# Two-block decode attention on one core: V loads three units behind K loads, the last four V in pieces, the final transpose and scaling split by batch

## The chip, the cores and the metric

The kernel runs on one core of one Trainium2 chip. The metric is the device time of the slowest core in microseconds (us); with one core that is this core's time. Every run quoted here is fast (the runs of each kernel lie within 1.5% of its fastest), and every kernel gave the reference's result. "Span" is the length of the one profiled execution; it is 1.75 to 3.25 us shorter than the time taken of that same execution.

## The reference, cut to what matters

```python
# block A; block B is the same with its own inputs.  B=2 batches, 32 heads, Sk=8192, Dh=192, D=640, bf16
q = (x @ wq).reshape(B, 1, 32, 192).transpose(0, 2, 1, 3)
scores = einsum("bhqd,bhkd->bhqk", q, k_cache) * 192 ** -0.5
o = einsum("bhqk,bhkd->bhqd", softmax(scores), v_cache)
return o.transpose(0, 2, 1, 3).reshape(B, 1, 32 * 192) @ wo
# ... output: the two blocks' results side by side
```

One query per batch and head meets 8192 keys and values: 837 MB have to be read and hardly anything is reused, so this is a streaming problem.

## The kernel before: what the change and the argument touch

The work is cut in 128 units (2 blocks x 32 heads x 2 batches). A unit loads one K and one V tile, each 128 partitions x 24,576 bytes (3 MB), into two buffers each. VectorE multiplies K with the query and sums 48 of the 64 columns; ScalarE sums the other 16 with its accumulator; GpSimd finds the maximum over the partitions; ScalarE takes the exponential into `pb`; TensorE multiplies it with V in 32 matmuls ("PV"). Each pair of heads is then transposed by TensorE (f3), scaled by ScalarE (f4) and projected by TensorE (f5). Weights come in 16 groups, each a `wq` and a `wo` load of 960 KB.

All loads go through one queue, in this order; a K load waits until its buffer's product is done, a V load until its buffer's PV is done:

```python
for u in range(NU):
    korder.append(("k", u))
    if u >= 1:
        korder.append(("v", u - 1))
korder.append(("v", NU - 1))
# ... weights of the next group go in between, at u % 8 == 2 (wo) and 3 (wq)
```

The steady part of three engines is a loop; ahead of it and behind it the code is straight:

```python
LOOPS = dict(dve=[(6, 8, 15)], act=[(4, 8, 15)], pe=[(7, 4, 13), (71, 4, 13)])   # first slot, slots a turn, turns
```

At the end the last K comes in two parts, the last V in four pieces, ScalarE takes 26 columns instead of 16 in the last unit, and ten idle matmuls are there, meant to keep TensorE's clock up (in the trace of this kernel they run from 1940.8 to 1942.9 us; the granted clock is at half from 1941.88 and again from 1952.12, for 3.41 us each; what they do isn't shown).

## Time and profile before

| | before |
|---|---|
| time, median of 3 runs | 1969.08 us (1968.56 to 1969.44) |
| span of the profiled run | 1967.1 us |
| VectorE busy | 84% |
| DMA rate in the steady part | 430 to 431 GB/s |
| last part of the last V lands | 1953.76 us |
| last landing to the end of the span | 13.34 us |

The landing times are from the trace's records of the load semaphores: the trace has 16 updates for each load, and the profile counts 16 DMA engines. This document reads each update as one engine's part of the load; the trace doesn't name the engine. The kernel waits for all 16.

The first view is the profile page of the kernel before: busy time by engine, the data rate in 40 equal slices of the span, and the queues (packets, MB, share of the 16 engines' time).

```profile
PE 1120.1 (57%) x5014; PEld 593.3 (30%) x5014; DVE 1655.3 (84%) x962; ACT 905.0 (46%) x4763; POOL 133.2 (7%) x269
...
GB/s 384 429 429 430 431 430 431 429 431 431 427 433 431 430 431 429 433 430 431 429 429 431 429 430 431 430 432 427 433 430 430 432 429 431 431 429 431 431 430 286
...
q8 instruction: 11, 0.18, 0.0%
q14 instruction: 13, 0.11, 0.0%
```

The rate stands at 430 from the second slice to the last but one. No engine is busy all the time; the transfer is the limit. Note the last two lines, which look like nothing: 24 packets with which engines fetched their own instructions.

The table by stretch of the kernel before, one stretch of it: busy time of each engine with its count of instructions, granted clock, DMA share, GB/s.

```profile
core 0: us, PE busy (x) PEld busy (x) DVE busy (x) ACT busy (x) POOL busy (x), PEclk, DMA share, GB/s
...
1700.00:1900.00 200.00, 116.69 (x523) 61.66 (x522) 171.20 (x100) 95.72 (x504) 9.59 (x26) 0.74 1.01 431
```

The end of the chain of waits of the kernel before: start, duration, what, each step released by the one above it.

```profile
1901.70 22.52 DMA kb<-in_B_k_cache_dram
...
1940.93 8.98 ACT prodA L301 x52
...
1951.51 0.45 ACT pb L308 x2
...
1952.01 7.05 PE ops L382 x32
1959.06 1.15 PE oTps L401 x12
...
1961.53 0.92 PE outps L417 x6
...
1962.48 0.43 ACT oTz L337 x2
...
1962.95 1.77 PE outps L417 x6
...
1964.75 0.43 ACT out_sb L347
```

The last K is followed by its scores, by ScalarE's 26 accumulations (52 instructions, 8.98 us) and by the exponential at 1951.51. Only then can the 32 PV matmuls start, at 1952.01; the last part of V lands at 1953.76, while they run. So 13.34 us of this kernel lie behind the last byte. That is what the change goes for.

### The profile page before, as it was taken

What the parts mean: (1) busy time and instruction counts of PE and PEld (TensorE: products, weight loads), DVE (VectorE), ACT (ScalarE), POOL (GpSimd) and SP (SyncE); (2) the same over time, 40 slices, a digit from 0 to 9 for tenths busy, and PEclk for the clock granted to TensorE, in tenths of its full rate; (3) what the DMA queues carried; (4) which work ended last, traced back from release to release, by engine and by line L of the source; (5) the groups of instructions that cost most, each with busy time, mean ns of one, the idle gap of its engine ahead of it and who ended that gap; (6) DMA issues with size and microseconds to landing.
All of it is one profiled execution on the core that took longest, in us unless ns stands there. A gap on an engine that the chain in (4) does not pass through costs nothing.

```text
span 1967.1 us, 18620 instructions
## 1 busy us (share of the span) xinstructions
PE 1120.1 (57%) x5014; PEld 593.3 (30%) x5014; DVE 1655.3 (84%) x962; ACT 905.0 (46%) x4763; POOL 133.2 (7%) x269
## 2 busy tenths in 40 slices
PE   2565555655555565555654666556554565556557
PEld 1232223333232232332332333223332232323234
DVE  7787888888888888888888888888788888888886
ACT  4444544445445444454445444444444444544544
POOL 4020000000000000000000000000000000000001
PEclk7776777777777777777777777777777777777777
DMA  9999999999999999999999999999999999999996
GB/s 384 429 429 430 431 430 431 429 431 431 427 433 431 430 431 429 433 430 431 429 429 431 429 430 431 430 432 427 433 430 430 432 429 431 431 429 431 431 430 286
DMA packets 55896, 837.08 MB, mean 426 GB/s; under 512 B 7352, under 2 KB 18240, under 8 KB 22976
## 3 DMA queue, kind: packets, MB, share of 16 engines
q1 hardware_dynamic: 55856, 836.79, 99.6%
q8 instruction: 11, 0.18, 0.0%
q14 instruction: 13, 0.11, 0.0%
q10 hardware_dynamic: 16, 0.01, 0.0%
HBM read 836.77 MB, written 0.01 MB: 425 GB/s over the span
## 4 chain that ended last, share of the span: by engine, by line
DMA 75%; DVE 18%; issue 5%; PE 1%; ACT 1%; POOL 0%; SPq 0%; ACTq 0%; DVEq 0%
DMA kb<-in_B_k_cache_dram 38%; DMA kb<-in_A_k_cache_dram 37%; DVE prodD L283 16%; DVE prodD L290 1%; DVE prodA L279 1%; ACT prodA L301 0%; PE ops L382 0%; POOL mg L266 0%; DVE sc L294 0%; PE outps L417 0%; PE oTps L401 0%; SPq L219 0%; SPq L226 0%; ACT pb L308 0%; ACT out_sb L347 0%
## 5 line engine op out<-in xcount | busy, mean ns | idle before, releaser
L382 PE MATMUL ops<-vb,pb 128*33 128x384 bf16 x4096 | 957.9, 409 | 837.1 <-DMA vb<-in_A_v_cache_dram 421.5
L382 PEld LDWEIGHTS ops<-vb,pb 128*33 128x33 bf16 x4096 | 482.8, 120 | 1312.5 <-issue 674.4
L301 ACT ACTIVATE prodA<-prodA 128x192 bf16<-128x192 bf16 x2058 | 712.4, 350 | 76.1 <-DVE prodA L279 75.6
L283 DVE TENSOR_TENSOR prodD<-kb,qbc 128x9216 bf16<-128x9216 bf16 x128 | 632.7, 4943 | 3.5 <-DMA kb<-in_A_k_cache_dram 3.5
L290 DVE TENSOR_TENSOR prodD<-prodD 128x4608 bf16<-128x4608 bf16 (+2 forms) x384 | 598.1, 1558 | 13.3
L279 DVE TENSOR_TENSOR prodA<-kb,qbc 128x3072 bf16<-128x3072 bf16 x128 | 226.3, 1768 | 254.6 <-DMA kb<-in_B_k_cache_dram 127.8
L301 ACT ACTIVATION_READ_ACCUMULATOR prodA<-prodA 128x1 f32 x2058 | 390.4, 190 | 0.0
L305 ACT ACTIVATE nb<-mg 128x1 f32<-128x1 f32 x128 | 25.9, 203 | 704.8 <-POOL mg L266 704.8
L294 DVE TENSOR_REDUCE sc<-prodD 128x48 f32<-128x1152 bf16 x128 | 172.9, 1351 | 4.4
L266 POOL PARTITION_ALL_REDUCE mg<-mp x128 | 53.2, 416 | 1690.9 <-DVE mp L286 1690.9
L315 ACT ACTIVATE o_sb<-ops 1x384 f32<-1x384 f32 x63 | 30.2, 479 | 131.2 <-PE oTps L390 112.0
L343 ACT ACTIVATE qbc<-qps 128x384 bf16<-128x384 f32 x64 | 31.4, 491 | 119.5 <-PE qps L365 119.4
L270 POOL PARTITION_ALL_REDUCE lall<-rs x128 | 70.5, 551 | 115.3 <-ACT pb L308 115.3
L390 PEld LDWEIGHTS oTps<-ones,o_sb 33*128 33x128 f32 x372 | 67.1, 257 | 9.8 <-issue 9.8
L390 PE MATMUL oTps<-ones,o_sb 33*128 33x1 f32 x372 | 69.7, 311 | 0.0
L308 ACT ACTIVATE pb<-sc,nb 128x64 bf16<-128x64 f32 x128 | 52.2, 408 | 16.6 <-ACT nb L305 6.3
L286 DVE TENSOR_REDUCE mp<-sc 128x1 f32<-128x64 f32 x128 | 28.2, 220 | 14.2 <-issue 4.3
L365 PE MATMUL qps<-wqs,xbc_0 128*128 (+1 forms) x160 | 32.4, 334 | 6.2 <-DMA wqs<-in_A_wq_dram 6.2
L365 PE MATMUL qps<-wqs,xbc_1 128*128 (+1 forms) x160 | 32.2, 333 | 0.6 <-ACT qbc L343 0.6
L417 PE MATMUL outps<-wos,oTz 128*4 (+1 forms) x192 | 32.0, 304 | 0.5 <-ACT oTz L337 0.5
L316 ACT ACTIVATE o_sb<-ops 1x384 f32<-1x384 f32 x63 | 30.4, 482 | 0.7
L308 ACT ACTIVATION_READ_ACCUMULATOR pb<-sc,nb 128x1 f32 x128 | 23.9, 186 | 0.0
(29 smaller groups left out, 87.1 us busy)
## 6 DMA issues: line engine op xcount, KB each, us to landing
vb<-in_A_v_cache_dram SPq DMA_DIRECT2D x64, 3072.0 KB, 22.2
kb<-in_A_k_cache_dram SPq DMA_DIRECT2D x63, 3072.0 KB, 22.5
kb<-in_B_k_cache_dram SPq DMA_DIRECT2D x63, 3072.0 KB, 22.5
vb<-in_B_v_cache_dram SPq DMA_DIRECT2D x62, 3072.0 KB, 22.1
wos<-in_A_wo_dram SPq DMA_DIRECT2D x8, 960.0 KB, 24.5
wqs<-in_B_wq_dram SPq DMA_DIRECT2D x8, 960.0 KB, 26.8
wos<-in_B_wo_dram SPq DMA_DIRECT2D x8, 960.0 KB, 24.4
wqs<-in_A_wq_dram SPq DMA_DIRECT2D x7, 960.0 KB, 26.8
```

Source lines behind the costliest of these rows:

```text
L266: return lambda eng: eng.partition_all_reduce(mg[u % 2][:], mp[u % 2][:], 128, bass.bass_isa.ReduceOp.max)
L270: return lambda eng: eng.partition_all_reduce(lall[g % 2][:, b:b + 1], rs[u % 2][:], 128, bass.bass_isa.ReduceOp.add)
L279: return lambda eng: eng.tensor_tensor(prodA[u % 2][:, 0:na, :], kb[u % NK][:, 0:na, :], qb_bc(u, na), ALU.mult)
L283: return lambda eng: eng.tensor_tensor(prodD[:, 0:T - na, :], kb[u % NK][:, na:T, :], qb_bc(u, T - na), ALU.mult)
L290: return lambda eng: eng.tensor_tensor(prodD[:, 0:nd, 0:w], prodD[:, 0:nd, 0:w], prodD[:, 0:nd, w:2 * w], ALU.add)
L294: return lambda eng: eng.tensor_reduce(sc[u % 2][:, na:T], prodD[:, 0:T - na, 0:24], AXL.X, ALU.add)
L301: return lambda eng: eng.activation(prodA[u % 2][:, t, :], prodA[u % 2][:, t, :], ACTF.Identity, accum_out=sc[u % 2][:, t:t + 1])
L308: return lambda eng: eng.activation(pb[u % 2][:, :, ::32], sc[u % 2][:].rearrange("p (j a) -> p j a", a=2), ACTF.Exp, bias=nb[u % 2][:], s ...
L365: ins = eng.matmul(qps[:, 0:QW], xbc[blk][b][:, c, :], wqs[:, slot, c, off].rearrange("p a n -> p (a n)") if slot is not w % 2 else wqs[:, ...
L382: ins = eng.matmul(ops[(u // B) % 2][0:33, b, 0:QW], pb[u % 2][:, j, :], vv[:, j, :], start=(j == 0), stop=(j == T // 2 - 1))
L390: ins = eng.matmul(oTps[:, 2 * i + b:2 * i + b + 1], o_sb[:, b, :, :].rearrange("p s (r i) -> p i (s r)", i=3)[:, i, :], ones33[:], start= ...
L417: ins = eng.matmul(outps[blk][0:4, 0:NH2], oTz[:, i, 2 - 2 * half:6 - 2 * half], wos[:, pr, i, half * NH2:(half + 1) * NH2], start=(first ...
```

## The change

Intent: let V trail K by three units, so that when the last bytes arrive they are V bytes whose scores are long done; cut the last V loads in pieces, so that only an eighth of one is left to multiply; split the last transpose and scaling by batch, so that batch 0's part is done early. The core of the diff (cuts marked):

```diff
-    NA_LAST = min(cfg.get("NA_LAST", 26), T - 2)
-    WARM = cfg.get("WARM", 10)
+    LAG = cfg.get("LAG", 3)
+    LATE = LAG - 1
+    NPB = 4
 ...
-    NA_MAX = max(NA_MAIN, NA_LAST)
+    NA_MAX = NA_MAIN                    # 16
 ...
-        pb = [sb(f"pb{i}", [128, T // 2, 33], BF16) for i in range(2)]
+        pb = [sb(f"pb{i}", [128, T // 2, 33], BF16) for i in range(NPB)]
 ...
+            for i, cuts in enumerate(((32, 64), (32, 64), (16, 32, 48, 64), (16, 32, 48, 56, 64))):
 ...  # the last four V loads, cut at these columns, one semaphore a piece
-        if NU >= 4:
-            KSPLIT[NU - 1] = k1sem
 ...
-                put(pe_tab, u, 0, pe_pv(u, 0, T // 2), w0 + [("v", u)], ("pv", u))
+                put(pe_tab, u + LATE, 0, pe_pv(u, 0, T // 2), w0 + [("v", u)], ("pv", u))
 ...  # f1, f3, f4, f5 move by LATE slots too
-                put(pe_tab, u1 + 2, 1, pe_f3h(1), [("f1", g1), ("f3a", pp)], ("f3", pp))
+                put(pe_tab, at - 1, 2, pe_f3h(1, (0,)), [("f1a", g1)], ("f3b", pp))
+                put(pe_tab, at, 1, pe_f3h(1, (1,)), [("f1", g1), ("f3b", pp)], ("f3", pp))
+                put(act_tab, at - 1, 4, act_f4(pp, (0,)), [("f3b", pp)] + w4, ("f4a", pp))
+                put(act_tab, at + 2, 3, act_f4(pp, (1,)), [("f3", pp), ("f4a", pp)] + w4, ("f4", pp))
 ...
-            if u >= 1:
-                korder.append(("v", u - 1))
-        korder.append(("v", NU - 1))
+            lag = min(1 + u // 8, LAG)
+            while u - lag >= nv:
+                korder.append(("v", nv))
+                nv += 1
+        for u in range(nv, NU):
+            korder.append(("v", u))
 ...
-                if u % UG == (2 if UG >= 8 else 1):
+                if u % UG == (5 if UG >= 8 else 1):
 ...  # the fixed LOOPS are replaced by a search for the longest repeating stretch
-                S_act.emit(eng, LOOPS["act"])
+                S_act.emit(eng, 8)
```

## The prediction

> **What bounds it.** DMA. The busy-by-stretch table shows 429 to 431 GB/s in every 200 us stretch from 100 to 1900 us, DMA share 1.00 to 1.01; DVE is 84% busy. [...] 837.08 MB at 430.5 GB/s is 1944.4 us of the 1967.1 us span. At most 22.7 us (1.2%) lie outside the stream, and the change cuts no bytes, so 2% is out of reach.
>
> **Before, outside the stream.** Head: bytes flow from about 3 us. Tail, from timeline and chain: the last K lands near 1937, the last exp ends at 1951.96. Only then 32 PV matmuls run (1952.0 to 1959.06), although V landed by about 1953 (bandwidth falls 313, 149, 123, 16 GB/s per us and is zero from 1954). Then transposes (2.4 us), the last-but-one projection (0.92), scaling (0.43), the last projection (1.77), copy (0.43), output DMA: 8.04 us from the last PV matmul to the span's end. Last byte (about 1953) to end: 14 us.
>
> **What the change does.** In the steady part nothing: V three units behind K leaves two buffers each; by my queue count about two loads stay in flight, and DVE (about 12.9 us per unit) fits the 14.6 us that the stream needs per unit. Four pb buffers let exp run ahead. PE and ACT reordering moves only work with slack. Early, PV of unit 1 now sits behind a Q projection that waits for the exp of unit 2; some 5 us of queued loads should cover that.
>
> At the end four V loads (29 us) follow the last K, so scores and exp (about 15 us) are hidden. After the last byte only the last piece remains, an eighth of V: 4 matmuls, 1.3 us at the cold interval of 0.32 us, 0.65 at the warm 0.16. [...] PV: 7.05 to about 1.4 us.
>
> The split of the transpose by batch gains little: in queue order the transposes of the other head and of batch 0 still come after the last PV (1.15 + 0.6 us), and on ScalarE the batch-0 scaling, which waits for them, stands BEFORE the batch-1 copy (0.65 us), which the last transpose needs. Copy, transpose (0.6), scaling (0.26) run in series; that eats what moving the 0.92 us projection saves. From the last PV to the end: about 8 us, as before.
>
> The stream may end 1 us earlier (1952.3) as the tail's 409 to 424 GB/s go to 430. End: 1952.3 + 1.4 + 8.1 = 1961.8 span, about 1963.6 timed.
>
> **Prediction: 1963.6 us (0.997 of before), 8 in 10 between 1960.5 and 1967.0. Faster by over 2%: 0.01; within: 0.98; slower: 0.01.**
>
> **Right if** bandwidth stays at 429 to 431; the last chain starts with a V load, not exp; four PV matmuls follow the last landing; the batch-0 scaling precedes the last copy on ScalarE; last byte to end is 9 to 10 us. **Wrong if** a hole shows in the bandwidth below 300 us (ramp of the lag) or before the last V loads (buffers freed late by a cold PE); the cold PE falls behind the last pieces (8 matmuls 2.6 us, a piece every 1.8 us); or the new order of addresses changes the HBM rate.

Two passages are cut from it where marked: a ceiling for the data rate and a rule for what lowers TensorE's clock. No run here shows either. No term of the sum goes with them: 1952.3 + 1.4 + 8.1 = 1961.8 us of span, about 1963.6 us timed. That the rate can't rise much over 430.5 GB/s, on which "2% is out of reach" also rests, was the author's estimate. The two intervals of the PV matmuls are in the trace of the kernel before: they start 0.320 us apart (median) where the granted clock is at half and 0.163 us apart where it is full.

## More of the kernel before

Buffers are laid out in SBUF one after the other, in the order in which they are made:

```python
kb = [sb(f"kb{i}", [128, T, Dh], BF16) for i in range(NK)]          # 2 x 24,576 bytes a partition
vb = [sb(f"vb{i}", [128, T, Dh], BF16) for i in range(NV)]
prodA = [sb(f"prodA{i}", [128, NA_MAX, Dh], BF16) for i in range(2)] # NA_MAX = 26, 384 bytes a column
prodD = sb("prodD", [128, ND_MAX, Dh], BF16)
# ... small tiles
pb = [sb(f"pb{i}", [128, T // 2, 33], BF16) for i in range(2)]       # 2,112 bytes each
# ... small tiles
wqs = sb("wqs", [128, 2, DC, HG * Dh], BF16)
wos = sb("wos", [128, HG, 3, D], BF16)
```

## The result, and the profile after

| | before | after |
|---|---|---|
| time, median of 4 runs each | 1968.82 us (1968.02 to 1969.44) | 1974.64 us (1973.90 to 1975.65) |
| span of the profiled run | 1967.1 us | 1973.2 us |
| last landing | 1953.76 us | 1963.63 us |
| last landing to the end | 13.34 us | 9.57 us |

The ratio is 1.003 (95% interval 1.0013 to 1.0048): within 2%, slower by 5.8 us, and outside the predicted range. Ratios in this document are the mean time of one kernel's fast runs over that of the other's fast runs of the same rounds, so they are not quite the ratio of the medians quoted beside them.

The end became 3.8 us shorter (13.34 - 9.57), as intended. But the last landing came 9.9 us later, with the same bytes. The page of the kernel after, lines as before:

```profile
GB/s 384 425 428 427 431 426 429 431 427 430 426 430 430 426 430 427 431 431 424 431 428 429 429 426 432 427 428 426 432 430 426 428 427 432 430 426 429 431 430 292
...
q8 instruction: 12, 0.20, 0.0%
q14 instruction: 17, 0.13, 0.0%
```

and one stretch of its table:

```profile
core 0: us, PE busy (x) PEld busy (x) DVE busy (x) ACT busy (x) POOL busy (x), PEclk, DMA share, GB/s
...
1700.00:1900.00 200.00, 116.12 (x520) 61.32 (x519) 171.33 (x102) 92.11 (x483) 9.89 (x27) 0.72 1.01 429
```

(The 17 packets on q14 hold one of 96 bytes at the very start; the trace has 16 fetches of 8 KB there, against 13 before. The 0.13 MB of the line show it, too.) The reader is to see how little it takes: 429 instead of 431 GB/s, many slices at 424 to 428, over the whole run. Half a per cent of 1950 us is 9.8 us. The engines' busy times are the same. No view of waits shows it, since the kernel waits for DMA before and after; one has to look at the DMA itself.

The end of the chain of the kernel after:

```profile
1933.71 14.67 DMA vb<-in_B_v_cache_dram
...
1948.43 2.78 PE ops L399 x16
1951.20 2.18 PE oTps L408 x12
1953.38 6.99 PE ops L399 x32
1960.37 0.91 PE outps L435 x6
1961.27 5.31 PE ops L399 x32
1966.58 1.36 PE oTps L419 x18
...
1967.96 0.27 ACT oTzL L353
...
1968.43 0.33 ACT o_sb L344
...
1968.81 0.70 PE oTps L419 x6
...
1969.53 0.28 ACT oTzL L353
...
1969.85 0.99 PE outps L435 x6
...
1970.87 0.43 ACT out_sb L363
```

The chain now comes from V, not from K and the exponential. But TensorE is behind: the PV of the last unit starts at 1961.27 with all its 32 matmuls still to do, not with the last 4, and ends at 1966.58, 2.95 us after the last landing at 1963.63. The stretches around it, in the table by stretch of the kernel after:

```profile
1942.00:1947.00 5.00, 4.01 (x26) 2.24 (x24) 3.99 (x6) 0.36 (x2) 0.35 (x1) 1.00 0.63 213
1947.00:1954.00 7.00, 6.17 (x37) 4.22 (x36) 0.16 (x1) 0.87 (x5) 0.38 (x1) 1.00 1.02 403
1954.00:1958.00 4.00, 4.00 (x16) 1.99 (x15) 0.00 (x0) 0.67 (x2) 0.00 (x0) 0.57 0.98 375
```

From 1954 to 1958 TensorE is busy 4.00 of 4 us, but with a granted clock of 0.57: 16 instructions. (The clock records of the trace have the clock at half from 1954.13 for 3.41 us.) Just ahead of it are the 12 fp32 transposes of one column each (1951.20, 2.18 us). And there is the hole in the rate, 213 GB/s from 1942 to 1947, that the prediction listed as a danger.

### Where the 9.9 us are: an account of the slowest DMA engine

An average of 16 engines hides it; take for each load the time from the previous load's last part to this load's last part.

| step on the slowest engine | before | after | times | sum of the differences |
|---|---|---|---|---|
| K or V load, 3072 KB (most of them) | 7.30 us | 7.30 us | | 0.2 us |
| `wq` load, 960 KB (median) | 2.32 us | 2.62 us | 15 | with `wo` |
| `wo` load, 960 KB (median) | 2.28 us | 2.40 us | 16 | 5.8 us |
| stalls: K or V loads over 7.42 us, excess summed | 2.94 us | 5.45 us | | 2.5 us |
| the rest, mostly the pieces at the end | | | | 1.3 us |

(5.8 is 6.38 us of excess after, less 0.54 before, each against a common 2.28 us; 1.3 is 9.87 less the three others.) With the 16 parts of each load sorted by landing, a weight load takes longer at every one of the 16 places (medians: `wq` 2.60 to 2.62 us after against 2.32 to 2.34 before, `wo` 2.40 to 2.41 against 2.27 to 2.29). In the kernel after, six of the stalls are single events of 0.66 to 1.02 us, and the others are smaller. The hole of 1942 to 1947 shows in the mean rate, but on the slowest engine the half loads that land at 1944.70 and 1948.38 took 3.67 and 3.69 us (half of 7.30 is 3.65) and the quarter loads behind them 1.85 to 1.9 us (a quarter is 1.83), so it cost next to nothing: the faster engines paused, the slowest one didn't.

This gave the first theory. **Theory A (addresses):** the SBUF addresses that the allocator gave differ. Before, `wqs` starts at byte 161,280 and `wos` at 176,640 of a partition, both multiples of 256. After, they start at 157,824 and 173,184, each 128 past a multiple of 256. (Two `prodA` of 10 x 384 bytes less, two `pb` of 2,112 bytes more: 3,456 bytes lower, which is 13.5 x 256.) K and V start 128 past a multiple of 256 in both kernels. If a start off such a multiple costs time, a cost by row fits the steps: the trace of the kernel before has 9,600 packets of 1,536 bytes for its 15 whole `wq` loads and 4,096 of 3,840 for its 16 `wo` loads, so 640 and 256 a load, or 40 and 16 rows for each of the 16 parts if they are equal, and 0.30 / 40 and 0.12 / 16 are both 7.5 ns. That is the author's estimate from these two steps; why a row should cost more no trace here shows. **Rival B (order):** the lag itself, or the new place of the weight loads in the queue, costs stream time. And for the stalls, later: **Theory C**, TensorE's instruction fetches, and **Theory D**, ScalarE's.

### The profile page after: what moved, and what is told of

Read it like the earlier page. It is cut to its first block, busy times and chain, and to the rows that moved or that the text cites. A ratio compares the mean times of both kernels' runs of the same rounds, so it can differ in the third digit from the quotient of the medians.

```text
span 1973.2 us, 18371 instructions
## 1 busy us (share of the span) xinstructions
PE 1116.4 (57%) x5004; PEld 591.5 (30%) x5004; DVE 1655.5 (84%) x962; ACT 904.1 (46%) x4743; POOL 152.7 (8%) x270
## 4 chain that ended last, share of the span: by engine, by line
DMA 72%; PE 22%; DVE 5%; issue 1%; SPq 0%; ACT 0%; DVEq 0%
DMA vb<-in_B_v_cache_dram 36%; DMA vb<-in_A_v_cache_dram 29%; PE ops L399 22%; DMA kb<-in_A_k_cache_dram 7%; DVE prodD L303 3%; DVE prodD L310 1%; DVE prodA L299 0%; DVE sc L314 0%; PE oTps L408 0%; PE oTps L419 0%; PE outps L435 0%; SPq L239 0%; SPq L246 0%; DVE mp L306 0%; ACT oTzL L353 0%
## 5 line engine op out<-in xcount | busy, mean ns | idle before, releaser
L286 POOL PARTITION_ALL_REDUCE mg<-mp x128 | 57.7, 451 | 1668.7 <-DVE mp L306 1668.7
L290 POOL PARTITION_ALL_REDUCE lall<-rs x128 | 84.2, 658 | 114.7 <-ACT pb L328 114.7
L381 PEld LDWEIGHTS qps<-wqs,xbc_1 128*128 128x128 bf16 x160 | 13.8, 102 | 58.9 <-ACT qbc L359 42.9
## 6 DMA issues: line engine op xcount, KB each, us to landing
wos<-in_A_wo_dram SPq DMA_DIRECT2D x8, 960.0 KB, 27.1
```

What stands on the lines that cost most here:

```text
L286: return lambda eng: eng.partition_all_reduce(mg[u % 2][:], mp[u % 2][:], 128, bass.bass_isa.ReduceOp.max)
L290: return lambda eng: eng.partition_all_reduce(lall[g % 2][:, b:b + 1], rs[u % 2][:], 128, bass.bass_isa.ReduceOp.add)
L381: ins = eng.matmul(qps[:, 0:QW], xbc[blk][b][:, c, :], wqs[:, slot, c, off].rearrange("p a n -> p (a n)") if slot is not w % 2 else wqs[:, ...
```

## The experiments

Both kernels have loops whose waits compare a semaphore with a value in a register (130 such waits before, 122 after). Every experiment is built on unrolled versions, `u_before` and `u_after`, which differ from the kernels in the loops alone; later on loops with constant waits were added. All runs have five rounds. The expectations were written ahead of each run. The kernel before ran beside each group: 1968.65, 1968.86, 1968.80, 1967.59 and 1968.86 us. Each group ran on another chip (the first and the third on the same), so runs of different groups are better compared by their ratios to it.

| run | what it is | us, median (lowest to highest) | ratio to before (95%) |
|---|---|---|---|
| u_before | before, unrolled | 1991.53 (1990.45 to 1991.80) | 1.0116 (1.0101 to 1.0131) |
| u_after | after, unrolled | 1995.34 (1993.28 to 1995.87) | 1.0135 (1.0120 to 1.0151) |
| ua_wpad | u_after, weights on 256 | 1987.20 (1986.43 to 1987.96) | 1.0097 (1.0082 to 1.0112) |
| ub_wmis | u_before, weights off 256 | 1999.77 (1997.35 to 2000.83) | 1.0158 (1.0144 to 1.0172) |
| ua_all | u_after, all large buffers on 256 | 1978.85 (1977.48 to 1979.64) | 1.0049 (1.0036 to 1.0063) |
| ub_all | u_before, all on 256 | 1983.20 (1982.55 to 1984.76) | 1.0077 (1.0063 to 1.0091) |
| ua_lag1 | ua_wpad with a lag of 1 | 1992.39 (1992.22 to 1993.35) | 1.0120 (1.0105 to 1.0136) |
| ua_tail | ua_wpad, end reordered | 1986.49 (1985.92 to 1987.88) | 1.0093 (1.0077 to 1.0108) |
| ua_loop | ua_all, TensorE in a loop | 1979.14 (1978.64 to 1991.89) | 1.0068 (1.0049 to 1.0087) |
| ua_pe16 | ua_all, TensorE instructions added | 1977.79 (1976.46 to 1979.45) | 1.0045 (1.0033 to 1.0058) |
| ua_e15 | ua_all, `wo` loads cut in two | 2094.51 (2089.00 to 2101.55) | 1.0646 (1.0628 to 1.0664) |
| ua_loop_tail | ua_loop, end reordered | 1977.94 (1976.63 to 1978.95) | 1.0048 (1.0035 to 1.0061) |
| ua_act16 | ua_all, ScalarE instructions added | 1989.82 (1988.69 to 1990.59) | 1.0112 (1.0097 to 1.0128) |
| ua_aloop | ua_all, ScalarE in a loop | 1962.85 (1962.77 to 1964.93) | 0.9976 (0.9963 to 0.9990) |
| ua_aloop_tail | ua_aloop, end reordered | 1961.57 (1961.14 to 1963.52) | 0.9969 (0.9956 to 0.9983) |
| ub_aloop | ub_all, ScalarE in a loop | 1968.13 (1966.76 to 1969.36) | 0.9997 (0.9984 to 1.0011) |
| ua_adloop_tail | ua_aloop_tail, VectorE in a loop too | 1960.21 (1960.19 to 1960.56) | 0.9958 (0.9944 to 0.9971) |
| u_after_adloop | u_after, ScalarE and VectorE in loops | 1975.56 (1974.94 to 1976.31) | 1.0034 (1.0021 to 1.0048) |

### First group: unrolling, and the weights' addresses both ways

u_before and u_after:

```diff
-        if NU == 128 and NBLK == 2:      # u_before: no loops
+        if False:
```
```diff
-                S_dve.emit(eng, 8)       # u_after: no loops; ScalarE and TensorE likewise
+                S_dve.emit(eng)
```

> A new base: the kernel before with its loops unrolled, so that every semaphore wait is against a constant (the loops' waits are against registers and may not be tried); nothing else differs. If instruction fetches cost stream time, as single stalls of 0.3 to 1.0 us on one DMA engine beside each 8 or 16 KB fetch suggest, the time rises by 2 to 8 us over before (about 1.2 MB of instructions, 2.8 us if spread evenly). If fetches are free, it stays within 0.5 us of before.

(Its 1.2 MB of instructions are an estimate: 18,620 instructions in the profile of the kernel before, at the 64 bytes each that ua_act16 shows below. The page of u_before has 0.64 + 0.42 = 1.06 MB.)

> The changed kernel with its loops unrolled, the base for undoing its parts. Theory A (6.3 us of the loss is the weight loads' SBUF addresses, the rest stalls and the tail): about 5 us slower than the unrolled before, and the weight loads still cost the slowest queue 2.62 us (wq) and 2.40 (wo) against 2.32 and 2.28 before. Theory B (the loss comes from the new loop structure, longer straight code and more fetches): it now equals the unrolled before within 1 us or beats it by the 3 to 5 us of the shorter tail.

Measured: unrolling costs 22.9 us in the old order (1991.53 against 1968.65) and about 20.7 us in the new one (1995.34 against 1974.64 of another group). That was a miss, far more than expected, and it turned out to be the way to the second cause: the stalls of the slowest engine, summed, grew from 2.9 us in the kernel before to 24.9 us in u_before. In the unrolled kernels the weight steps are as in their originals: 2.32 and 2.28 us in u_before, 2.61 and 2.40 us in u_after.

ua_wpad and ub_wmis put the same 128-byte tile ahead of the weight buffers. In the one it repairs the alignment, in the other it spoils it:

```diff
+        padw = sb("padw", [128, 32], F32)      # 128 bytes a partition
         wqs = sb("wqs", [128, 2, DC, HG * Dh], BF16)
         wos = sb("wos", [128, HG, 3, D], BF16)
```

> The unrolled changed kernel plus one unused 128-byte SBUF tile ahead of wqs, nothing else: wqs and wos then start at multiples of 256 bytes, as before the change; in the changed kernel they start 128 bytes off. Theory A (start address of the destination costs about 8 ns for each row of a descriptor): 6 us faster than the unrolled changed kernel (5 to 7.5), the wq step back to 2.32 us, wo to 2.28. Rival (order of K and V loads, lag of three units, or wo's new place in the queue): no change within 1 us, steps stay at 2.62 and 2.40.

> The unrolled kernel before plus the same 128-byte tile ahead of wqs, which moves wqs and wos to 128 bytes past a multiple of 256. Theory A: 6 us slower than the unrolled before (5 to 7.5), wq step 2.62 us, wo 2.40, with no change of order at all. Rival: the same time within 1 us.

Measured: ua_wpad is 8.1 us faster than u_after (1987.20 against 1995.34); ub_wmis is 8.2 us slower than u_before (1999.77 against 1991.53). The weight steps follow the addresses: 2.32 and 2.28 us in ua_wpad, 2.57 and 2.40 us in ub_wmis. Both are above the 5 to 7.5 us that were expected. In the profiled runs the last landing moves by 6.7 and 6.9 us, of which the weight steps make 6.2 and 5.6; in ua_wpad another 1.8 us come from the end (9.4 us in u_after, 7.6 in ua_wpad), where the half clock didn't fall on the 32 PV matmuls of the last but one unit (5.38 us instead of 6.99). Theory A holds both ways, with nothing else changed but the place of a few small tiles behind the weights, and it isn't the order: ua_wpad has the new order and the old steps. The old and the new order with the same alignment (ua_wpad against u_before) differ by 4.3 us in favour of the new one. In ua_wpad `wqs` starts at 157,952, which is a multiple of 256 but not of 512; offsets other than 0 and 128 weren't tried.

### Second group: K and V on the boundary too, the lag alone, the end alone

ua_all puts the tile ahead of the first K buffer, so that K, V and the weights all start on a multiple of 256 (ub_all does the same, with a second tile ahead of `wqs`, which the first would have moved off):

```diff
+        padk = sb("padk", [128, 32], F32)
         kb = [sb(f"kb{i}", [128, T, Dh], BF16) for i in range(NK)]
```

> The unrolled changed kernel with the unused 128-byte tile ahead of the K buffers instead of ahead of wqs: now K, V, wqs and wos all start at multiples of 256 bytes (K and V start 128 off in both kernels of the study). Theory A, extended: if a row of 24576 bytes that starts off a multiple of 256 also costs about 8 ns more, a K or V load of 8 rows for each DMA engine shrinks from 7.30 to 7.24 us; 256 of them make 16 us (12 to 18) less than ua_wpad, about 1971 us, and the stream runs at 433 to 434 GB/s instead of 430. Rival (430 is the ceiling of the fabric or of HBM, and start addresses matter for short rows only): the same as ua_wpad within 1.5 us.

> The unrolled kernel before with K, V, wqs and wos at multiples of 256 bytes (its weights were there already, its K and V were not). Theory A, extended: 16 us (12 to 18) under the unrolled before, about 1975.5. Rival: no change. If this holds too, the address explains the pace in both orders of the loads.

Measured: ua_all is 8.35 us faster than ua_wpad, ub_all 8.3 us faster than u_before (the groups differ; by the ratios to before it is 9.4 and 7.7 us). The direction was right, the size half of what was expected. A K or V step falls from 7.30 to 7.265 us, and 0.035 us over 8 rows of 24,576 bytes is 4.3 ns a row, not 7.5. The misplacement of K and V is older than the change; it was there to be had in the kernel before as well.

ua_lag1 is rival B's test:

```diff
-    LAG = cfg.get("LAG", 3)
+    LAG = cfg.get("LAG", 1)
```

> ua_wpad with the lag of V set back from three units to one (everything else of the change kept). If the lag is what shortens the end: the scores of the last unit come after the stream again, 10 us slower than ua_wpad (7 to 13), with the exp of the last unit on the chain of waits. If the lag itself costs stream time in the steady part: the same or faster than ua_wpad in landing of the last load, by more than 1 us.

Measured: 5.2 us slower than ua_wpad, below the 7 to 13 us that were expected. Its last landing is at 1977.98 us of its span, that of ua_wpad at 1976.98, so the lag costs the stream nothing; nor does the new place of the weight loads cost more than 0.8 us, since u_before, with the old order and the same alignment as ua_wpad, has its last landing at 1976.19. From the last landing to the end it takes 13.5 us, against 7.6 us in ua_wpad. Rival B falls; the gain of the lag is real and lies where the change meant it to lie.

ua_tail moves the next to last pair's transposes, scaling and projection one slot earlier and batch 0's last transposes between the last V pieces:

```diff
-                put(pe_tab, at - 1, 1, pe_f3h(0), ...
+                put(pe_tab, at - 2, -0.5, pe_f3h(0), ...
-                put(pe_tab, at - 1, 2, pe_f3h(1, (0,)), [("f1a", g1)], ("f3b", pp))
+                put(pe_tab, at - 2, 0.25, pe_f3h(1, (0,)), [("f1a", g1)], ("f3b", pp))
 ...  # f3, f4 and f5 of the pair before it one slot earlier, too
```

> ua_wpad with the end reordered only: the last-but-one pair's transposes, scaling and projection move ahead of the last V loads' matmuls, the last pair's transposes of the first head and of batch 0 move ahead of the last pieces, and the batch-0 scaling comes before its waits can hold up the batch-1 copy. If PE's backlog and the ScalarE order are what remain after the last byte: 4 us faster than ua_wpad (2 to 5), last landing to end 6 to 7 us instead of 9.6. If the end is bound by the landing alone: within 1 us.

Measured: 0.7 us faster than ua_wpad, a miss (expected 4). In ua_wpad there is little to gain: the PV of its last unit ends 0.9 us after the last landing, against 2.95 us in the kernel after, and from the last landing to the end it is 7.6 us there and 6.8 us in ua_tail. Why is only argued: one DMA engine is behind the other fifteen (by 9.9 to 12.3 us in the load of ua_all that is listed below), so V trickles in late. That can't be all of it, since u_after is unrolled too, with the same 51 fetches on q14, and its last PV ends 2.4 us after the last landing.

### Third group: which engine's instruction fetches?

The stalls of the unrolled kernels sum to some 25 us, and nearly each follows an instruction fetch by a few us. The number of fetches rose with unrolling, from 11 to 39 on q8 (16 KB each) and from 13 to 51 on q14 (8 KB each). Theory C had q8, TensorE's, as the cause. ua_loop puts TensorE's steady part in a loop. To wait for constants it uses semaphores of its own that are set back after each wait, and the engine that is waited for raises them:

```diff
         for sem, val in need:
-            eng.wait_ge(sem, val)
+            if id(sem) in self.clear:
+                eng.wait_ge(sem, self.clear[id(sem)])      # a constant
+                eng.sem_clear(sem)
+            else:
+                eng.wait_ge(sem, val)
 ...
-                S_pe.emit(eng)
+                S_pe.emit(eng, 4)
```

ua_pe16 adds 16 one-column matmuls to each of the first 124 units:

```diff
+                for _ in range(16 if (j0, j1) == (0, T // 2) else 0):
+                    eng.matmul(ops[(u // B) % 2][0:33, b, 400:401], wdl[:], wdl[:, 0:1], start=True, stop=True)
```

> ua_all with TensorE's steady part in a loop again (3,300 fewer instruction records in its program; its waits are against constants on semaphores that are set back), the other engines still unrolled. Theory C (each 16 KB fetch of TensorE's instructions lands on one DMA engine and holds every K and V load up by about 0.67 us, as all loads wait for their slowest part): fetches fall from 39 to about 12, so 27 x 0.67 = 18 us less than ua_all (14 to 22), about 1961 us, under the kernel before. Rival (unrolling costs time otherwise, by ScalarE's and VectorE's code or the waits): within 3 us of ua_all.

> ua_all with 16 one-column matmuls more in each of the first 124 units (TensorE idles half the time; about 3970 more instructions, 15.5 fetches of 16 KB more). Theory C: 15.5 x 0.67 = 10 us slower than ua_all (8 to 13). Rival (fetches are free): within 1.5 us.

Measured: ua_loop 1979.14 us (one of its 6 runs took 1991.89; the others lie close together) and ua_pe16 1977.79 us, against ua_all's 1978.85. The fetches on q8 went from 39 to 13 and to 54. The sum of the stalls didn't move (25.9 us in ua_loop). Some 3,970 instructions more (ua_pe16) made 15 fetches more and a time 1.1 us shorter; 26 fetches fewer (ua_loop) made it 0.3 us longer. Theory C falls: TensorE's fetches, twice as large, are free here, where another engine is far behind anyhow. A look at the fetch times would have told: of the 41 stalls over 0.25 us in ua_all's trace, 35 land within 9 us after a fetch on q14 and 8 within 9 us after one on q8.

ua_e15 was meant to take one DMA engine out of the `wo` loads, to find the engine that is hit:

```diff
-                    S_sp.add(sp_wo(w), waits=[key("f5", (w - 1) * HG // 2)])
+                    S_sp.add(sp_wo(w, 0, 120), waits=[key("f5", (w - 1) * HG // 2)])
+                    S_sp.add(sp_wo(w, 120, 128))
```

> ua_all with each wo load cut into 120 and 8 partitions. [...] If one engine paces the stream: 15 to 27 us faster when it is the last of the 16 (it is rid of 16 x 2.28 us)[...]. If the stream is limited by all engines together: within 3 us of ua_all, slower.

(Cut from it, where marked: which engines serve the 120 and the 8 partitions, which no run shows, and two forecasts that rested on that alone. That the engine which is left out is the last of the 16 is the author's assumption; the trace has 15 updates for the one piece and 8 for the other, and doesn't name the engines.)

Measured: 2094.51 us, 116 us slower than ua_all, which is 7.2 us for each of the 16 `wo` loads. On the slowest engine a `wo` step takes 5.05 us instead of 2.29, and the K and V loads that land just ahead of it take up to 11 us instead of 7.26. Each cut load has 15 and 8 updates that come with the data. The cut itself costs so much that the question it was to answer stayed unanswered. Why it costs so much isn't known either.

ua_loop_tail is ua_loop with the reordered end.

> ua_loop with the end reordered as in ua_tail. In ua_tail the gain was small because the slow engine's lag of 12 us let TensorE catch up; with the loop the lag is 5 us or less, as in the kernel before, so TensorE's backlog counts: 2 to 5 us faster than ua_loop, last landing to end 6.5 us. If the backlog is not what counts: within 1 us of ua_loop.

Measured: 1.2 us faster than ua_loop, below the 2 to 5 us that were expected. (TensorE's loop hadn't taken the lag of the slow engine away: the stalls of ua_loop sum to 25.9 us.)

### Fourth group: ScalarE's fetches

On q14, most of the fetches of ua_all come 47 to 58 us apart. With 128 instructions to 8 KB, which ua_act16 below shows (2,048 instructions more, 16 fetches of 8 KB more), that is what ScalarE gets through: 16 accumulations a unit, two instructions each, and a few more. Theory D: each of these lands on the DMA engine that is the slowest anyhow and holds the whole stream up. Its packet takes 0.31 us in the trace, the stall behind it is about 0.65 us long. ua_act16 adds 2,048 instructions to ScalarE; ua_aloop puts ScalarE's steady part alone in a loop, in the way shown for TensorE (period 8 slots, 14 turns).

```diff
+            for i in range(16 * (u % 4), 16 * (u % 4) + 16):        # ua_act16, once a unit
+                ins = eng.activation(actx[0:1, i:i + 1], ones33[0:1, 0:1], ACTF.Identity)
```
```diff
-                S_act.emit(eng)          # ua_aloop; constant waits, own semaphores set back as above,
+                S_act.emit(eng, 8)       # raised by a drain behind the instruction that is waited for
```

> ua_all with 16 one-element ScalarE instructions more in every unit: 2048 more, at 128 instructions to an 8 KB fetch some 16 fetches more on queue q14 (51 to about 67). Theory D (each fetch of ScalarE's instructions lands on the slowest DMA engine and holds the K and V stream up by about 0.65 us): 16 x 0.65 = 10 us more than ua_all, about 1989 us, and the sum of the stalls of the slowest engine grows by about 10 us from 25. Rival R (the stalls come from something else that unrolling brings, or from VectorE's fetches): within 1.5 us of ua_all's 1979.

> ua_all with ScalarE alone in a loop, with constant waits; TensorE, VectorE and GpSimd stay unrolled (TensorE and VectorE even get drain instructions more, 140 and 224). Theory D: fetches on q14 fall from 51 to about 20, some 32 of them ScalarE's, so 32 x 0.65 = 21 us less than ua_all: about 1958 us, faster than both the kernel before (1968.8) and after (1974.6). Rival R: about 1979, as with TensorE's loop.

The queue lines of the pages. First ua_all, the reference:

```profile
q8 instruction: 39, 0.64, 0.1%
q14 instruction: 51, 0.42, 0.0%
```

then ua_act16:

```profile
q8 instruction: 39, 0.64, 0.1%
q14 instruction: 68, 0.55, 0.1%
```

and ua_aloop:

```profile
q8 instruction: 40, 0.66, 0.1%
q14 instruction: 24, 0.20, 0.0%
```

Measured: 16 fetches more (the 68th packet of ua_act16 has 96 bytes) cost 11.0 us (1989.82 against 1978.85), 0.69 us each; the sum of the stalls rises from 27.1 to 36.0 us. 27 fetches fewer give back 16.0 us (1962.85), 0.59 us each; the stalls fall to 9.2 us. ua_all ran in another group; by the ratios to before it is 12.4 and 14.4 us, 0.78 and 0.53 us each. Theory D holds, both ways, at about the size that it named for the first and at two thirds to three quarters for the second. And 38 fetches more at 0.6 us is 23 us, which is what unrolling cost.

The landings show what such a fetch does. Below are the 16 parts of one V or K load near 1700 us, in us before the last part:

```
before    V  -4.37 -4.21 -3.71 -3.05 -2.46 -2.30 -2.25 -2.20 -2.17 -2.03 -2.01 -1.90 -1.23 -0.77 -0.13  0.00
after     K  -4.78 -4.67 -4.17 -3.81 -3.08 -3.01 -2.93 -2.92 -2.89 -2.88 -2.45 -2.39 -2.36 -2.16 -1.01  0.00
ua_all    V -12.29 -12.25 -12.21 -12.00 -11.91 -11.90 -11.89 -11.41 -11.03 -10.75 -10.74 -10.35 -10.14 -9.94 -9.92  0.00
ua_aloop  V  -7.86 -7.83 -7.70 -7.33 -6.53 -6.16 -4.09 -2.06 -1.97 -1.88 -1.87 -1.82 -1.82 -0.39 -0.24  0.00
```

In ua_all fifteen engines are some 10 us ahead and one comes last. The author's reading: a K or V load is 128 packets of 24,576 bytes (32,256 for the 252 whole loads of the kernel before) and 16 updates in the trace; if an equal share goes to each engine, the extra work of one engine isn't made up by the others: they run ahead until the buffers are full (9.9 to 12.3 us ahead here), and from then on the one sets the pace. With ScalarE's fetches gone the last three engines are within 0.4 us of each other. Which of the 16 serves which queue the trace doesn't record; that they differ is inferred from q8's fetches costing nothing in ua_loop and ua_pe16 while q14's cost all.

> ua_aloop with the reordered end (transposes, scaling and projection of the next to last pair of heads earlier, batch 0's transposes of the last pair ahead of the last V pieces). Theory D: 1 to 3 us below ua_aloop, about 1956 us, because in a stream without the lag of one engine TensorE is again behind at the end, as it was in the kernel after by some 3 us. Rival R: about 1978, as ua_loop_tail.

Measured: 1961.57 us, 1.3 us less than ua_aloop, within the range expected for the difference (the absolute 1956 was missed, as ua_aloop's 1958 was). The runs of the two overlap, so the times alone don't show it; in the traces the stretch from the last landing to the end falls from 8.6 to 6.8 us.

> The kernel before with all large buffers on multiples of 256 bytes and ScalarE in a constant-wait loop: the same two side effects taken away from the old order of loads. Theory D: 21 us below ub_all's 1983.2, about 1962 us. Against ua_aloop of the same call it tells what the change itself is worth when addresses and fetches are the same: 3 to 5 us in favour of the new order (ua_all was 4.35 below ub_all). Rival R: about 1983.

Measured: 1968.13 us, 15.1 us below ub_all instead of the 21 expected. Against it ua_aloop is 5.3 us faster, with the same alignment and nearly as many fetches on q14 (24 against 21). That is the change's own worth, and the prediction's value for it was 5.5 us (1969.08 - 1963.6).

### Fifth group: closing the account

In ua_aloop 9.2 us of stalls are left; from 850 us on they come about every 183 us (12.5 units) and each follows a fetch that comes as often, which fits 128 of VectorE's instructions (the number that ua_act16 shows for ScalarE). ua_adloop_tail puts VectorE in such a loop as well. u_after_adloop does it without the 128-byte tile: the change's own addresses and end, few fetches.

```diff
-                S_dve.emit(eng)
+                S_dve.emit(eng, 8)
```
```diff
-        padk = sb("padk", [128, 32], F32)      # u_after_adloop only
```

> ua_aloop_tail with VectorE in a constant-wait loop too. In ua_aloop the stalls that are left come every 183 us, behind fetches that come as often: 12.5 units, which is 128 of VectorE's instructions. Theory D: with ScalarE's fetches gone the DMA engine that takes VectorE's is now among the slowest, so taking these away too (24 fetches on q14 to about 15) brings the sum of stalls from 9.4 to about 4.5 us and the time from 1961.6 to about 1957 us. Rival: VectorE's fetches cost nothing, as they did while ScalarE's were there: about 1961.

> The kernel after with its own addresses (no 128-byte tile), ScalarE and VectorE in constant-wait loops, the end as in the change. It should close the account: with few fetches and the misplaced buffers it ought to be the kernel after again, about 1974 us (ua_adloop_tail's 1957, plus 1.3 for the end, plus 8.1 for the weights and 8.35 for K and V, as measured in unrolled kernels). If the cost of the addresses were one of unrolled kernels only, it would be within 3 us of ua_adloop_tail.

Measured: ua_adloop_tail 1960.21 us, 1.4 us less than ua_aloop_tail (of another group; by the ratios to before it is 0.9958 against 0.9969, 2.2 us), with 18 fetches on q14. Expected were 4.6 us. The stalls behind VectorE's fetches are gone, but three others of 1.1 to 1.5 us stay, at 868, 1255 and 1651 us, with no fetch on q14 just ahead of them. Each comes 4 to 6 us after a fetch of TensorE's on q8, the 17th, 25th and 33rd of 40, and u_after_adloop has stalls behind the same three. The first of the 40 has one behind it as well, the other 36 none above 0.25 us. So it looks as if a few of TensorE's fetches do cost time once ScalarE's are gone; why these, and whether they are the cause, is open. It is the fastest kernel: 8.65 us below the kernel before, 14.4 us below the kernel after, and still not a gain of 2%.

u_after_adloop 1975.56 us, expected 1974: with the bad addresses put back and 18 fetches on q14 it is the kernel after again (1974.64 us, 16 fetches on q14), though it has 40 fetches on q8 where the kernel after has 12. So addresses cost some 14 us in a kernel with few fetches as well (1975.56 less 1960.21, less 1.3 for the reordered end), of which the part for K and V was there before the change.

## Why the prediction was wrong

- "What bounds it: DMA", and 2% out of reach: held. No version here gained 2%: the steady rate is 430 to 431 GB/s in the kernel before, and 429 to 433 from the third slice to the last but one of the fastest (ua_adloop_tail). How much higher it could go isn't shown. Over so long a stream half a per cent of rate (9.8 us) outweighs the 3.8 us that were saved at the end.
- **"In the steady part nothing": this is the step that failed.** The argument was about who waits for whom (buffers, slack of VectorE, two loads in flight), and that part was right: ua_lag1 shows that the lag costs no stream time. But the change altered two things that no wait shows. First, the weight buffers moved off a multiple of 256 bytes: 5.8 us by the account of the steps, and 8.1 and 8.2 us when undone and done in unrolled kernels (6.7 and 6.9 us by the last landing). Second, ScalarE's straight code around its loop grew (the compiled program from 700 to 985 instructions, 2.2 fetches of 128), and q14 made 16 fetches instead of 13: 3 x 0.65 us is 2.0 us, and the account has 2.5 us more of stalls. Of the second the cost per fetch is shown by experiment; that these fetches cost it in the kernel after is worked out from it and from the times of the stalls (fetches at 178, 220, 1845, 1892 and 1939 us, stalls of 0.66 to 0.70 us in loads that land 2 to 8 us later), not run alone.
- "The stream may end 1 us earlier (1952.3)": failed for the same reason. It ended at 1963.63, 9.9 us later than before.
- "PV: 7.05 to about 1.4 us": failed, by the cause listed under "wrong if": TensorE fell behind. All 32 matmuls of the last unit ran after 1961.27, behind a stretch with a granted clock of 0.57, and ended 2.95 us after the last landing. The half clock is some 1.7 us of it (the 32 matmuls of the unit before took 6.99 us, the last 32 took 5.31); the transposes (2.18 us) and the projection (0.91 us) that stand between the last V pieces are the rest of the backlog. (The clock fell, at 1954.13, while the profile has TensorE busy, after twelve one-column transposes. How busy the array itself was in them the profile doesn't say, and what lowers the clock isn't shown.) That the remedy is small is shown by the reordered end: 1.3 us in ua_aloop_tail.
- "From the last PV to the end: about 8 us": it was 6.6 us (1966.58 to 1973.2). Two sizes were off in opposite directions, 1.5 us each, so the sum "9 to 10 us" from last byte to end held by luck: 9.57. A sum that holds doesn't prove its terms.
- "The batch-0 scaling precedes the last copy on ScalarE": held. It stands at 1967.96 us, the copy at 1968.23 and 1968.43.
- "A hole below 300 us or before the last V loads": a hole came (213 GB/s, 1942 to 1947), but cost next to nothing, since the slowest engine had no hole.
- "The new order of addresses changes the HBM rate": the nearest of the listed dangers. It was an address, but the one in SBUF, and it could have been computed before the run, from the sizes of the buffers.

In sums: +5.8 (weights) + 2.5 (stalls) + 0.2 + 1.3 (pieces and rest) - 3.8 (end) = +6.0 us of span, measured 6.1. Most of the predicted 5.5 us was there once these were taken away: 4.3 us in the pair with only the weights aligned, 4.35 us with all aligned, 5.3 us with ScalarE looped. They were paid back, and more, by things that nobody had changed on purpose.

## What to carry to other kernels

When a kernel is bound by a DMA stream, look at the start address of every DMA target before and after a change in any buffer's size. In this case a start 128 bytes past a multiple of 256 cost 8.1 and 8.2 us for the weights (ua_wpad, ub_wmis) and 8.35 and 8.3 us for K and V (ua_all, ub_all), against a start on a multiple; other offsets weren't tried. Count instruction fetches per queue on the page, by the MB (the packets can include a tiny one): a share of "0.0%" can be 1% of the time (q14 of ua_all has that share, and 27 fetches fewer took 16.0 us off its 1978.85), since a load is there only when its last part has come, which in ua_all is 9.9 us behind the other fifteen. ScalarE's loop was worth more here (16.0 us) than the better schedule (5.3 us, ua_aloop against ub_aloop). And read a stream by its slowest engine, from the landings of the 16 parts, rather than from the mean rate: 429 against 431 GB/s is all that the mean shows of the 9.9 us.
